# Masks on GpSimd for two of six units, squares on ScalarE, and late gathers one tile at a time, in a block-sparse attention with an expert router

## Chip, cores and metric

The kernel runs on one core of a Trainium2 chip. The metric is the device time of one execution in microseconds, as the median of several runs. A core has TensorE (PE; its weight loads are shown as PEld), VectorE (DVE), ScalarE (ACT), GpSimd (POOL) and SyncE (SP), which issues most DMAs.

## The reference, cut to what matters

Attention over 4 batches, 8 heads, 768 positions and head size 64, with a block mask, and then a router with 8 experts over the 3072 rows of 512 that it gives.

```python
scores = scale * q @ k.T                       # per batch and head, 768 x 768
scores = np.where(mask, scores, -1e9)          # mask by blocks of 32: window, first, last, random
attn = exp(scores - max) / (sum + 1e-9)
x = attn @ v                                   # -> (3072, 512)
xn = x / (norm(x) + 1e-6);  logits = xn @ en.T / tau
e = argmax(logits);  gate = softmax(logits)[e]
out = gate * (relu(x @ w1[e]) @ w2[e])         # w1: 512 x 1024, w2: 1024 x 512
```

## The kernel before

**Attention.** The work goes by pairs of heads: 16 pairs (4 per batch, index `g`), each of two halves of 384 queries, each half of six *units* `u` of 128 keys; `kc = u % 6`. Six units make one half `w = u // 6`; there are 192 units and 32 halves. For a unit, `score_fast` puts scores of both heads, keys on partitions, into PSUM: four bf16 matmuls add the mask (`kmask` by `qmask`, line 368, 0 or -1e9), and four groups of f32 matmuls add the product of `kt` and `qt` (line 368 too). ScalarE takes the exp of the 128x768 scores into a tile `e` (line 371; no maximum is subtracted, and a test at the end falls back to an exact version where sums are out of range). `attend_fast` multiplies `e` with `v` into `av` (line 390), and VectorE adds the `e` of a half up into `esum` (lines 385 and 387). At `kc` 5 ScalarE copies one half of `av` out (`part`, line 394) and VectorE adds the other (`at`, line 396).

Within a step, unit `u` is attended and then unit `u + 2` scored; at `kc` 0 the score comes first. The PSUM pool of scores has two buffers, the pool of `e` four.

`settle(w)` turns a half back to rows: small matmuls of `at` with an identity and the expert embedding (line 418), and of `esum` with ones for the row sums (line 425), into one PSUM tile `back`; VectorE adds the two halves of the sums (line 428), adds 1e-9 (429), takes the reciprocal (433), and writes the normed rows `x` (435) and the logits `part` (438). It is called at `kc` 3 of the following half. `squares(w)` at `kc` 4 squares and adds up 384 columns on GpSimd, one multiply (line 449) and seven adds of halving width (line 453); the last half uses ScalarE (line 463). The transposes of the next pair's `k` and `q` are VectorE operations at the first two units of a pair (line 285).

After each batch, steps of `route` (norms, logits, argmax, gate: lines 502 to 560) and `rank` are run between units at the places that `after_sequence` lists.

**Experts.** Rows are grouped by expert into tiles of 128. Five tiles (`NE`) are made of the first two batches, while attention still runs; the others ("late" tiles) after all rows are ranked. A tile is `hp = xgt @ w1` (line 891), relu by ScalarE for one half and VectorE for the other (894, 898), `yp = h @ w2` (904), scaling by the gate (912), and a scatter to the output by an indirect DMA from GpSimd's queue (913). The rows of a late tile are gathered by four indirect DMAs on that queue (line 812), two tiles ahead: `fetch(i)` calls `fetch_rows(i + 2)`. Weights come through SP's queue, 2 MB each (line 841).

In the first expert tile, `last_rows` settles the last half and routes the last batch in the middle of the tile. `between` then ranks and makes the slots of the late tiles in steps: `fill_slots` gives `slot_l` and, with four more matmuls (line 672), the indices `quarter` of the gathers.

The framework schedules each engine's instructions in program order by priority; `issue_after(x)` keeps what follows behind instruction `x`.

Of the kernel before, what the change touches and what calls it, by code (L numbers as in the profile page):

```python
# [19 lines left out]
P = 128  # L20
# [29 lines left out]
DEN_LOW, DEN_HIGH = 0.1, 1e10  # L50
NEG = -1.0e9


# [304 lines left out]
def score_fast(k, u):  # L358

    nc = k.nc  # L360
    g, qh, kc = u // (2 * NC), u // NC % 2, u % NC
    kt, qt = k.turned[g]
    ps = k.big.tile([P, 2, 512], F32, name="sc", tag="big")
    queries = slice(qh * HALF, (qh + 1) * HALF)
    quarters = [(h, r, slice(kc * P + D * r, kc * P + D * (r + 1))) for r in range(2) for h in range(2)]
    for rows, cols, first in ((k.kmask, k.qmask, True), (kt, qt, False)):
        for h, r, keys in quarters:
            nc.tensor.matmul(ps[D * r:D * (r + 1), h, 0:HALF], lhsT=rows[D * h:D * (h + 1), keys],  # L368
                             rhs=cols[D * h:D * (h + 1), queries], start=first, stop=not first)
    e = k.ep.tile([P, 2, HALF], F32, name="e", tag="e")  # L370
    k.exps = nc.scalar.activation(e, ps[:, :, 0:HALF], ACT.Exp, scale=SCALE)  # L371
    k.es[u] = e


# [25 lines left out]
def settle(k, w):  # L400
# [26 lines left out]
    den = k.dens[:, w, :]  # L427
    nc.vector.reduce_sum(out=den.rearrange("p (t h) -> p t h", t=NQ), in_=sums, axis=AX.X)
    nc.vector.tensor_scalar(out=den, in0=den, scalar1=1e-9, scalar2=None, op0=ALU.add)

# [11 lines left out]
def squares(k, w):  # L442

    nc = k.nc
    b, j, qh = w // (2 * NPAIR), w // 2 % NPAIR, w % 2
    chunks = slice(qh * NQ, (qh + 1) * NQ)
    x = k.x[b][:, chunks, j, 0:P]
    sq = k.sp.tile([P, NQ, P], F32, name="sq", tag="sq", bufs=1)
    nc.gpsimd.tensor_tensor(out=sq, in0=x, in1=x, op=ALU.mult)  # L449
    width = P // 2  # L450
    while width:
        out = sq[:, :, 0:width] if width > 1 else k.nsq[b][:, chunks, j:j + 1]
        k.squared = nc.gpsimd.tensor_tensor(out=out, in0=sq[:, :, 0:width], in1=sq[:, :, width:2 * width],  # L453
                                            op=ALU.add).ins
        width //= 2


def last_squares(k, w):

    b, j, qh = w // (2 * NPAIR), w // 2 % NPAIR, w % 2  # L460
    for c in range(qh * NQ, (qh + 1) * NQ):
        sq = k.sp.tile([P, P], F32, name="sq_l", tag="sq_l")
        k.nc.scalar.activation(sq, k.x[b][:, c, j, 0:P], ACT.Square,
                               accum_out=k.nsq[b][:, c, j:j + 1])
# [187 lines left out]

def fill_slots(k, lanes, val, nt, tiles, name, quarters=False):

    nc, p = k.nc, k.dp
    both = two_banks(k, "slot_ps")
    ps = both[:, 0, 0:2 * tiles]
    for t in range(nt):
# [7 lines left out]
    nc.vector.tensor_copy(out=slot, in_=got)  # L666
    if not quarters:
        return slot

    ps = both[:, 1, 0:NG * tiles].rearrange("p (g t) -> p g t", g=NG)  # L670
    for g in range(NG):
        nc.tensor.matmul(ps[:, g], lhsT=k.spread[:, g].rearrange("p e t -> p (e t)"), rhs=got, start=True, stop=True)
    k.quarter = k.const.tile([P, NG, tiles], I32, name="quarter")
    nc.vector.tensor_scalar(out=k.quarter, in0=ps, scalar1=float(ND), scalar2=k.group[:, 0:1], op0=ALU.mult,
                            op1=ALU.add)
    return slot

# [37 lines left out]
def dispatch_late(k):  # L715
# [63 lines left out]
    yield  # L779
    k.slots.append(fill_slots(k, k.lanes, val, NT, NL, "slot_l", True))  # L780
    yield
# [18 lines left out]
def fetch_rows(k, i):  # L800
# [5 lines left out]
    with ExitStack() as order:  # L806
        if k.squared is not None and not late:
            order.enter_context(k.tc.issue_after(k.squared))
        if late:
# [35 lines left out]
def fetch(k, i):  # L845

    if i + 2 < NE + NL:
        fetch_rows(k, i + 2)
    need = [(t, at) for t in range(NE + NL) for at in parts(t)]
    begin = [t for t, _ in need].index(i)  # L850
    for t, at in need[k.loads:begin + 3]:
        for _ in fetch_weights(k, t, at):
            pass
# [26 lines left out]

def expert_tile(k, i, meanwhile=None):
    nc = k.nc
# [4 lines left out]
    for f0 in (0, half):  # L887
# [5 lines left out]
        if f0 == 0:  # L893
            nc.scalar.activation(h[:, 0:half], hp, ACT.Relu)  # L894
            if meanwhile:
                meanwhile()
        else:
            k.relu = nc.vector.tensor_scalar(out=h[:, half:NF], in0=hp, scalar1=0.0, scalar2=None, op0=ALU.max).ins  # L898

    if i + 1 < NE + NL:  # L900
# [7 lines left out]
def finish(k, i, yp, gate, slot):  # L908
# [3 lines left out]
    nc.vector.tensor_scalar(out=y, in0=yp, scalar1=gate, scalar2=None, op0=ALU.mult)  # L912
    nc.gpsimd.indirect_dma_start(  # L913
        out=k.out[:, :], out_offset=bass.IndirectOffsetOnAxis(ap=slot, axis=0),
        in_=y[:, :], in_offset=None, bounds_check=N - 1, oob_is_err=False,
    )

# [56 lines left out]
def attention_fast(n, ctx):  # L974
# [3 lines left out]
    n.acc, n.big = pool("acc", 1, space=PSUM), pool("big_f", 2, space=PSUM)  # L978
    n.ld, n.tp, n.ep = pool("ld", 3), pool("tp", 2), pool("ep", 4)
    pairs = B * NPAIR  # L980
# [26 lines left out]
    load_pair(n, 1, (2,))  # L1007
    plan, experts = [], build_experts(n)
    for u in range(units):
        g = u // per  # L1010
        if u % per == 0 and g + 2 < pairs:
            load_pair(n, g + 2, (2,))
        if u % NC == 3 and NC < u < units - 2 * NC:
            settle(n, u // NC - 1)
        if u % NC == 4 and NC < u < units - 2 * NC:
            squares(n, u // NC - 1)
        if u in (2, 4, 7):
# [6 lines left out]
        for when, what in plan:  # L1024
            if when == u % (per * NPAIR):
                with n.tc.issue_after(n.summed.ins), n.tc.issue_after(n.exps.ins), n.tc.issue_after(n.tick.ins):
                    what()

        steps = [partial(attend_fast, n, u)] + ([partial(score_fast, n, u + 2)] if u + 2 < units else [])
        for step in reversed(steps) if u % NC == 0 else steps:  # L1030
            step()
        turn = u % per - (0 if g else NC - 1)
        if turn in (0, 1) and g + 1 < pairs:
# [45 lines left out]

def expert_tiles(n, between=(), first=None):  # L1080
    between = iter(between)
    for i in range(NE + NU):
# [6 lines left out]
        else:  # L1089
            expert_tile(n, i, first if i == 0 else None)  # L1090
        next(between, None)
    used = n.nc.values_load(n.used[0:1, 0:1], min_val=0, max_val=NL)
    with ExitStack() as more:
        for i in range(NU, NL):
            more.enter_context(n.tc.If(used > i))
            fetch(n, NE + i)
            expert_tile(n, NE + i)


def fast(n):  # L1100
    n.rings, n.loads, n.squared = {}, 0, None
    with ExitStack() as ctx:
# [10 lines left out]
        def between():  # L1113
            rank(n, B - 1)
            late = dispatch_late(n)
            next(late)
            yield
            yield
            next(late)
            count_good(n)  # L1120
            yield

        def last_rows():
            settle(n, 2 * B * NPAIR - 1)
            last_squares(n, 2 * B * NPAIR - 1)
            for _ in route(n, B - 1):
                pass

        expert_tiles(n, between(), last_rows)

# [92 lines left out]
```

## Time and profile before

| what | value |
|---|---|
| median of 3 runs | 697.7 us (697.24 to 698.05) |
| profiled execution, its own time | 701.82 us |
| span from first to last instruction in it | 700.1 us |
| granted TensorE clock, mean | 0.995 |
| attention ends about | 324 us |
| late expert tiles start about | 405 us |

The profile has, for groups of instructions by line and shape, the busy time, the mean of one in ns, and the engine's idle time before them with what ended it. The timeline has a start, a length (to the end of the last of the instructions merged in that line), the engine, the line, what is written and read, the number of instructions, and in brackets the idle time before it and its releaser. A table of stretches has for each engine the busy time and, in brackets, the instructions: PE, PEld, DVE, ACT, POOL, then the granted clock, the share of the DMA engines and GB/s. Matmuls of the four quadrants of the array run side by side, so a matmul's length is more than its share of TensorE's time.

### The profile page before, as it was taken

The page shows a single profiled execution, that of the slowest core. Times are in us where ns is not written, and L with a number is a line of the kernel's source. Part 1 is how long each engine was busy: PE and PEld are TensorE (multiplying, and loading weights), DVE is VectorE, ACT ScalarE, POOL GpSimd, SP SyncE. Part 2 cuts the span into 40 slices and gives each one's busy share as a digit, 9 for nine tenths or more (in the row PEclk, how much of TensorE's full clock was granted, in tenths as well). Part 3 has the DMA queues.
Part 4 walks back from the last instruction along what each step waited for, and adds up shares of the span by engine and source line. Part 5 has one row for each costly group of instructions (what it writes and reads, how often), then busy time and mean ns, then how long its engine had stood idle before and what let it go on. Part 6 is the DMA issues. An engine that isn't in the chain of part 4 may idle for free.

```text
span 700.1 us, 19413 instructions
## 1 busy us (share of the span) xinstructions
PE 683.5 (98%) x8237; PEld 449.7 (64%) x8237; DVE 345.2 (49%) x733; ACT 188.4 (27%) x266; POOL 296.3 (42%) x450
## 2 busy tenths in 40 slices
PE   9999999999999999999999899999999999999993
PEld 4777777555555555557767677766476665767771
DVE  6887778878788888765661111221112111221111
ACT  5455555554555455553000000000000001000000
POOL 1355466544774468535405543244323432241121
PEclk9999999999999999999999999999999999999997
DMA  7733344575326769643998799999899998999991
GB/s 122 131 66 52 49 70 70 131 161 100 64 41 163 128 159 209 225 153 132 329 408 306 284 402 322 342 349 336 291 390 414 404 377 303 418 396 416 326 330 51
DMA packets 172650, 164.87 MB, mean 235 GB/s; under 512 B 129340, under 2 KB 129340, under 8 KB 169478
## 3 DMA queue, kind: packets, MB, share of 16 engines
q1 hardware_dynamic: 165734, 149.86, 68.1%
q0 software_dynamic: 5216, 13.43, 5.4%
q8 instruction: 68, 1.11, 0.7%
q10 hardware_dynamic: 1600, 0.20, 0.2%
q14 instruction: 32, 0.26, 0.1%
HBM read 147.66 MB, written 16.07 MB: 234 GB/s over the span
## 4 chain that ended last, share of the span: by engine, by line
PE 93%; issue 2%; another core or an unknown queue 1%; DVE 1%; POOL 1%; ACT 0%; POOLq 0%
PE sc L368 22%; PE hp L891 21%; PE yp L904 21%; PE av L390 18%; PE back L425 3%; PE hp L932 2%; PE yp L952 2%; PE back L418 2%; PE warm L81 1%; POOL xg L812 0%; DVE row L938 0%; POOL nrm L514 0%; PE hp L944 0%; DVE h L898 0%
## 5 line engine op out<-in xcount | busy, mean ns | idle before, releaser
L371 ACT ACTIVATE e<-sc 128x768 f32<-128x768 f32 x192 | 155.5, 810 | 149.1 <-PE sc L368 147.3
L891 PEld LDWEIGHTS hp<-xgt,w 128*128 128x128 f32 x1472 | 168.1, 192 | 13.2 <-issue 12.6
L891 PE MATMUL hp<-xgt,w 128*128 128x128 f32 x1472 | 169.9, 276 | 2.0 <-issue 2.0
L904 PE MATMUL yp<-w,h 128*128 128x512 f32 x368 | 162.3, 593 | 1.2 <-DVE h L898 1.2
L368 PE MATMUL sc<-qt,kt 64*64 64x384 f32 x1536 | 162.7, 482 | 0.0
L390 PE MATMUL av<-e,vld 64*64 64x384 f32 x1536 | 158.9, 486 | 0.0
L812 POOL DMA_INDIRECT xg<-x_dram,quarter x88 | 88.2, 1003 | 140.4 <-DVE gate L877 101.5
L387 DVE TENSOR_TENSOR esum<-esum,e 128x768 f32<-128x768 f32 x128 | 129.3, 1010 | 34.4 <-ACT e L371 30.6
L904 PEld LDWEIGHTS yp<-w,h 128*128 128x128 f32 x368 | 68.0, 190 | 78.9 <-issue 75.8
L453 POOL TENSOR_TENSOR sq<-sq 128x192 f32<-128x192 f32 (+1 forms) x186 | 103.3, 555 | 13.9
L894 ACT ACTIVATE h<-hp 128x512 f32<-128x512 f32 x23 | 13.7, 597 | 295.9 <-PE hp L891 282.5
L390 PEld LDWEIGHTS av<-e,vld 64*64 64x64 f32 x1536 | 62.4, 133 | 47.2 <-issue 18.2
L368 PEld LDWEIGHTS sc<-qt,kt 64*64 64x64 f32 x1536 | 65.2, 133 | 32.3 <-issue 25.1
L898 DVE TENSOR_SCALAR h<-hp 128x512 f32<-128x512 f32 x23 | 15.9, 691 | 131.6 <-PE hp L891 122.0
L449 POOL TENSOR_TENSOR sq<-x 128x384 f32<-128x384 f32 x31 | 28.4, 918 | 115.6 <-DVE part L438 97.7
L368 PE MATMUL sc<-qmask,kmask 64*64 64x384 bf16 x768 | 71.6, 323 | 0.1
L912 DVE TENSOR_SCALAR y<-yp,gate 128x512 f32<-128x512 f32 x20 | 15.0, 751 | 101.0 <-PE yp L904 88.8
L368 PEld LDWEIGHTS <-kmask 64*64 64x64 bf16 x768 | 30.3, 107 | 27.4 <-issue 23.1
L913 POOL DMA_INDIRECT out_dram<-y,slot_l x20 | 20.2, 1009 | 63.0 <-DVE y L912 57.7
L385 DVE TENSOR_TENSOR esum<-e 128x768 f32<-128x768 f32 x32 | 31.3, 979 | 7.1 <-ACT e L371 7.0
L425 PE MATMUL back<-ones,esum 64*64 64x1 f32 x1536 | 27.4, 190 | 0.0
L425 PEld LDWEIGHTS back<-ones,esum 64*64 64x64 f32 x1536 | 26.5, 135 | 0.0
(204 smaller groups left out, 366.7 us busy)
## 6 DMA issues: line engine op xcount, KB each, us to landing
w<-in_moe_w_dram SPq DMA_DIRECT2D x54, 2048.0 KB
w<-in_moe_w_dram SPq DMA_DIRECT2D x16, 512.0 KB
x_dram<-x SPq DMA_DIRECT2D x24, 258.0 KB
vld<-in_v_dram SPq DMA_DIRECT2D x32, 192.0 KB
kld<-in_k_dram SPq DMA_DIRECT2D x60, 96.0 KB
qld<-in_q_dram SPq DMA_DIRECT2D x60, 96.0 KB
x_early<-x SPq DMA_DIRECT2D x12, 258.0 KB
xg<-x_dram,quarter POOLq DMA_INDIRECT x88
```

The lines of the kernel that those rows point to most:

```text
L368: nc.tensor.matmul(ps[D * r:D * (r + 1), h, 0:HALF], lhsT=rows[D * h:D * (h + 1), keys], rhs=cols[D * h:D * (h + 1), queries], start=first ...
L371: k.exps = nc.scalar.activation(e, ps[:, :, 0:HALF], ACT.Exp, scale=SCALE)
L385: k.summed = nc.vector.tensor_tensor(out=k.esum, in0=k.first, in1=e, op=ALU.add)
L387: k.summed = nc.vector.tensor_tensor(out=k.esum, in0=k.esum, in1=e, op=ALU.add)
L390: nc.tensor.matmul(k.av[D * h:D * (h + 1), r, 0:HALF], lhsT=v[D * r:D * (r + 1), h, kc, :], rhs=e[D * r:D * (r + 1), h, :], start=(kc == 0 ...
L425: nc.tensor.matmul(sums[D * s:D * (s + 1), t, h, r:r + 1], lhsT=esum[D * r:D * (r + 1), h, cols], rhs=k.ones[D * r:D * (r + 1), 0:1], star ...
L449: nc.gpsimd.tensor_tensor(out=sq, in0=x, in1=x, op=ALU.mult)
L453: k.squared = nc.gpsimd.tensor_tensor(out=out, in0=sq[:, :, 0:width], in1=sq[:, :, width:2 * width], op=ALU.add).ins
L812: k.nc.gpsimd.indirect_dma_start(out=x[:, g], out_offset=None, in_=quarters, in_offset=bass.IndirectOffsetOnAxis(ap=k.quarter[:, g, t:t + ...
L891: nc.tensor.matmul(hp[:, f, :], lhsT=w1[:, d, (f0 + f) * P:(f0 + f + 1) * P], rhs=xt[:, d, :], start=(d == 0), stop=(d == ND - 1))
L904: nc.tensor.matmul(yp, lhsT=h[:, f, :], rhs=w2[:, f, :], start=(f == 0), stop=(f == NF - 1))
L913: nc.gpsimd.indirect_dma_start(out=k.out[:, :], out_offset=bass.IndirectOffsetOnAxis(ap=slot, axis=0), in_=y[:, :], in_offset=None, bounds ...
```

## The change

- **Masks.** In units with `kc` 2 or 5, from the second pair on and except seven listed in `WHOLE`, the mask matmuls are left out. Instead GpSimd multiplies `e` in place by a 0/1 mask `cut` in bf16. `build_cut` makes this mask once, in the first half, from the same matmuls and a Relu. This makes 53 of 192 units.
- **Order.** Scores run three units ahead (`AHEAD`), the pool of `e` has five buffers, and `settle` comes at `kc` 2.
- **Squares** of all halves are three ScalarE operations with an accumulator, at `kc` 5.
- **Row sums.** The two halves of the sums are added by an addition of 1e-9 to the first and one of the second, both read from PSUM, in place of a reduction and an addition.
- **Late gathers.** The gathers of a late tile are issued after the latest scatter; those of the first late tile in the middle of expert tile 3, right after `spread_slots`, which is what was the second part of `fill_slots`.
- **Last route.** The routing of the last batch is put behind the VectorE relu of the first expert tile.

The core of the diff:

```diff
+AHEAD = 3
+CUT = (2, 5)
+WHOLE = {1: (11, 20), 2: (11, 20), 3: (11, 14, 20)}
...
 def score_fast(k, u):
...
-    for rows, cols, first in ((k.kmask, k.qmask, True), (kt, qt, False)):
+    cut = g > 0 and kc in CUT and u % (2 * NC * NPAIR) not in WHOLE.get(g // NPAIR, ())
+    for rows, cols, first in ((k.kmask, k.qmask, True), (kt, qt, False))[int(cut):]:
         for h, r, keys in quarters:
             nc.tensor.matmul(ps[D * r:D * (r + 1), h, 0:HALF], lhsT=rows[D * h:D * (h + 1), keys],
-                             rhs=cols[D * h:D * (h + 1), queries], start=first, stop=not first)
+                             rhs=cols[D * h:D * (h + 1), queries], start=first or cut, stop=not first)
...
+    if cut:
+        mask = k.cut[:, CUT.index(kc), queries].unsqueeze(1).broadcast_to([P, 2, HALF])
+        k.squared = nc.gpsimd.tensor_tensor(out=e, in0=e, in1=mask, op=ALU.mult).ins
     k.es[u] = e
+
+def build_cut(k, i):
...
+            nc.tensor.matmul(ps[D * r:D * (r + 1), h, 0:HALF],
+                             lhsT=k.kmask[rows, CUT[i] * P + D * r:CUT[i] * P + D * (r + 1)],
+                             rhs=k.qmask[rows, h * HALF:(h + 1) * HALF], start=True, stop=True)
+    nc.scalar.activation(k.cut[:, i].rearrange("p (h t) -> p h t", h=2), ps[:, :, 0:HALF], ACT.Relu, bias=1.0,
+                         scale=-10.0 / NEG)
...
 def settle(k, w):
...
-    nc.vector.reduce_sum(out=den.rearrange("p (t h) -> p t h", t=NQ), in_=sums, axis=AX.X)
-    nc.vector.tensor_scalar(out=den, in0=den, scalar1=1e-9, scalar2=None, op0=ALU.add)
+    per_row = den.rearrange("p (t h) -> p t h", t=NQ)
+    nc.vector.tensor_scalar(out=per_row, in0=sums[:, :, :, 0], scalar1=1e-9, scalar2=None, op0=ALU.add)
+    nc.vector.tensor_tensor(out=per_row, in0=sums[:, :, :, 1], in1=per_row, op=ALU.add)
...
 def squares(k, w):
...
-    nc.gpsimd.tensor_tensor(out=sq, in0=x, in1=x, op=ALU.mult)
-    width = P // 2
-    while width:
...
     for c in range(qh * NQ, (qh + 1) * NQ):
+        sq = k.sp.tile([P, P], F32, name="sq", tag="sq")
         k.nc.scalar.activation(sq, k.x[b][:, c, j, 0:P], ACT.Square,
                                accum_out=k.nsq[b][:, c, j:j + 1])
...
 def fetch_rows(k, i):
...
-        if k.squared is not None and not late:
-            order.enter_context(k.tc.issue_after(k.squared))
+        behind = k.scattered if late else k.squared
+        if behind is not None:
+            order.enter_context(k.tc.issue_after(behind))
...
 def fetch(k, i):
-    if i + 2 < NE + NL:
+    if i + 2 < NE + NL and i + 2 != NE:
         fetch_rows(k, i + 2)
...
 def finish(k, i, yp, gate, slot):
-    nc.gpsimd.indirect_dma_start(
+    k.scattered = nc.gpsimd.indirect_dma_start(
...
 def attention_fast(n, ctx):
-    n.ld, n.tp, n.ep = pool("ld", 3), pool("tp", 2), pool("ep", 4)
+    n.ld, n.tp, n.ep = pool("ld", 3), pool("tp", 2), pool("ep", 5)
...
-        if u % NC == 3 and NC < u < units - 2 * NC:
+        if (u % NC == 2 and u > 2 * NC or u == NC + 3) and u < units - 2 * NC:
             settle(n, u // NC - 1)
-        if u % NC == 4 and NC < u < units - 2 * NC:
-            squares(n, u // NC - 1)
+        if u in (3, 5):
+            build_cut(n, u // 2 - 1)
...
-        steps = [partial(attend_fast, n, u)] + ([partial(score_fast, n, u + 2)] if u + 2 < units else [])
+        scored = u + (AHEAD if u > NC else 2)
+        steps = [partial(attend_fast, n, u)] + [partial(score_fast, n, i) for i in range(ahead, min(scored + 1, units))]
+        ahead = scored + 1
...
+        if u % NC == 5 and NC < u < units - 2 * NC:
+            with n.tc.issue_after(n.exps.ins):
+                squares(n, u // NC - 1)
...
 def expert_tiles(n, between=(), first=None, then=None, spread=None):
+    def first_late():
+        if spread:
+            spread()
+        fetch_rows(n, NE)
...
-            expert_tile(n, i, first if i == 0 else None)
+            expert_tile(n, i, {0: first, NE - 2: first_late}.get(i), then if i == 0 else None)
...
         def last_rows():
             settle(n, 2 * B * NPAIR - 1)
-            last_squares(n, 2 * B * NPAIR - 1)
-            for _ in route(n, B - 1):
-                pass
+            squares(n, 2 * B * NPAIR - 1)
+        def last_route():
+            with n.tc.issue_after(n.relu):
+                for _ in route(n, B - 1):
+                    pass
```

## The prediction

> **What bounds the kernel now.** I read the engine totals first, then busy time by stretch, then TensorE's instructions in order of time in one steady stretch.
>
> ```profile
> PE 683.5 (98%) x8237; PEld 449.7 (64%) x8237; DVE 345.2 (49%) x733; ACT 188.4 (27%) x266; POOL 296.3 (42%) x450
> ...
> 20.00:330.00 310.00, 310.00 (x6050) 196.34 (x6043) 244.90 (x479) 160.79 (x218) 171.49 (x299) 1.00 0.53 113
> ...
> 370.00:405.00 35.00, 32.09 (x202) 23.17 (x201) 5.88 (x15) 1.19 (x2) 20.98 (x21) 1.00 0.81 294
> ```
>
> In the attention stretch (20 to 330 us) PE is busy without a gap; VectorE (third number) is busy 79%, ScalarE 52%, GpSimd 55%. Only PE work removed, or PE work delayed, moves the time there. Around 370 to 405 PE has 2.9 us of holes; later it is full again.
>
> ```profile
> 154.36 0.83 PE L368 MATMUL sc<-qt,kt 64*64 64x384 f32 x8
> 155.01 0.83 PE L390 MATMUL av<-e,vld 64*64 64x384 f32 x8
> 155.65 0.34 PE L368 MATMUL sc<-qmask,kmask 64*64 64x384 bf16 x4
> 155.82 0.82 PE L368 MATMUL sc<-qt,kt 64*64 64x384 f32 x8
> 156.46 0.34 PE L368 MATMUL sc<-qmask,kmask 64*64 64x384 bf16 x4
> ```
>
> The second column (time from first start to last end) overlaps with the next group; the price of a group is the distance between starts. A mask is 155.82-155.65 = 0.16 us, a score 0.645, an av 0.645. A settle takes 1.04 (back starts 151.03, the next av 152.07). Six units and a settle are 6x(0.645+0.645+0.16)+1.04 = 9.74; the trace shows 9.79 (two like av groups start at 157.27 and 167.06).
>
> Then the two engines that get and lose work:
>
> ```profile
> 154.54 0.83 POOL L449 TENSOR_TENSOR sq<-x 128x384 f32<-128x384 f32 x1 [5.17 <-DVE part L438]
> 154.71 1.47 DVE L387 TENSOR_TENSOR esum<-esum,e 128x768 f32<-128x768 f32 x1 [0.20 <-ACT e L371]
> ...
> 254.11 0.95 DVE L387 TENSOR_TENSOR esum<-esum,e 128x768 f32<-128x768 f32 x1
> 254.22 1.52 POOL L449 TENSOR_TENSOR sq<-x 128x384 f32<-128x384 f32 x1 [5.86 <-DVE part L438]
> ```
>
> The same two instructions take 0.83 and 0.95 when first and 1.52 and 1.47 when second: whoever comes second waits for the other's end (154.54+0.83 = 155.37; esum ends 0.81 after that).
>
> **What the Trainium skill says.** "SBUF — State Buffer", section "Who interferes with whom": a VectorE instruction with two SBUF inputs and a GpSimd instruction that reads SBUF exclude each other for the whole instruction; one with at most one SBUF input does not. The lines above agree. The settle's and at's VectorE work reads one side from PSUM; only the five esum adds of a period contend. "GPSIMD Engine Reference", section "3.1 Elementwise — side-by-side cycle accounting": about 2.6 cycles per element for two inputs; at its 1.2 GHz 768 elements are an estimated 1.66 us, about 1.8 with a fixed part. The trace is split: the in-place adds of L453 fit (192 elements 0.59 alone, 96 elements 0.38: 2.2 ns each), the multiply L449 does not (384 in 0.83).
>
> **The change, part by part.** The order of instructions of both programs, engine by engine, gives the counts.
>
> *Masks.* 53 units (26 with kc 2, 27 with kc 5) lose their mask matmuls: 53x0.16 = -8.5 us of PE. Building the 0/1 mask costs two groups of four such matmuls, +0.3; its two Relu of 128x768 (0.81 each like L371) lie on an idle ScalarE. In exchange 53 multiplies of 128x768 go to GpSimd, between exp and av. Their price is not in the trace. Low end, from the nearest row, L449 (a multiply of full rows): twice 0.83 less the fixed part (0.14, what an op that queued behind a lock saves) = 1.51. High end, the slope of L453: 768x2.2 ns + 0.17 = 1.85. I take 1.51, for it is the same operation; L453 adds in place. In-place writing and the bf16 mask could push it up.
>
> Does it fit? Scores now run three units ahead. Call 0 the start of the av of unit 5; exp starts 0.25 after its score (155.01 to 155.26) and takes 0.81, a successor starts 0.04 later, PE needs about 0.2 from release to first product (weights 0.15). Unit 2: score ends 1.29, multiply ready 2.39, av due 5.23, so 2.6 us are free. Unit 5: score ends 6.52, ready 7.62, av due 9.42: **1.60 us** free. 1.51 fits, barely, and only where no esum holds the port.
>
> VectorE's order in a period: at, esum of 0+1, esum 2, 3, 4, the five settle operations (1.31), esum 5; esums follow each other every 1.05 (0.95 and a gap). In a period without transposes: at 1.46-2.02, esum 0+1 to 3.0, multiply 2 waits for it and runs to 4.4, esum 2, 3, 4 end at 5.4, 6.4, 7.5, multiply 5 runs 7.62-9.13 under the settle: no stall. Every other period has four transposes (2.06): multiply 2 goes first (2.39-3.9), esum 0+1 ends 4.7, transposes to 5.75, esum 3 ends 7.8; multiply 5 waits for it, ends 9.2, PE is just in time. But esum 4, the settle and esum 5 end 2.9 us into the next period; there at, multiply 2 and all esums are late, esum 4 runs 7.25-8.2, multiply 5 ends 9.56, and av starts 9.78: 0.36 late. So 0.18 on average, 27x0.18 = +4.9. Ends: 0, if the port is luckier; at 1.85 the same working gives stalls of 0.25 to 1.0, mean 0.63, 27x0.63 = +17. Net of masks: -8.5+0.3+4.9 = **-3.3** (-8.2 to +8.8).
>
> *Squares.* The GpSimd chain of L449 and L453 (about 4.2 us per period) becomes three ScalarE squares, 1.0 us together by the last rows' L463 (first start 332.11, last end 333.10). They sit behind exp 2 and delay exp 3 to 4.16; its av is due after 5.9 and the next user of its PSUM buffer starts at 5.88: 0, covered by 1.7 us; uncovered 1 us per period. ScalarE goes to 6x0.81+0.47+1.0 = 6.3 of 9.4. Without this GpSimd could not hold two multiplies.
>
> *Row sums, settle sooner, fifth e buffer.* Two tiny VectorE operations replace two (L428 0.164, L429 0.165): 0. The settle moves ahead of av 2; it needs at (2.02, or 3.6 when late) and starts at 4.19: 0, and it is what gives unit 2 its slack. If VectorE fell 2 us later still, PE would wait for at. Five e buffers keep the distance between an exp and the esum it overwrites: 0.
>
> *Last route after the relu.* In tile 0 PE waited 0.3 for h L898, queued behind routing on VectorE: -0.3. The route then ends about 0.7 later; its oh was ready 2.5 us before the rank matmul (338.57 against 341.09): covered.
>
> *Gathers.* SP's queue is unchanged in order. On GpSimd, the late gathers (1.3 us from start to start) stood 14 in a row, from 373.89 to 391.86, ahead of the scatter of tile 3. Now four are issued, then a scatter, then four. The first four move from 373.9 to about 376.5, and are first used at 398.74: covered by over 15 us. What they free:
>
> ```profile
> 383.88 0.69 DVE L898 TENSOR_SCALAR h<-hp 128x512 f32<-128x512 f32 x1 [9.56 <-remote]
> ...
> 384.63 3.70 PE L904 MATMUL yp<-w,h 128*128 128x512 f32 x8 [0.94 <-DVE h L898]
> ...
> 392.39 0.47 PE L891 MATMUL hp<-xgt,w 128*128 128x128 f32 x2 [1.04 <-issue]
> 393.80 4.29 PE L891 MATMUL hp<-xgt,w 128*128 128x128 f32 x37 [0.94 <-issue]
> ```
>
> PE's three holes (last brackets) are 2.9 us. They lie within the row of 14, and later tiles, with four gathers each, have none. The cause is not named ("remote"), so this is a choice: **-2.9**, between 0 and -4.0 (hp of tiles 3, 4 and 5 starts at 371.43, 388.33, 404.96: two tiles of 16.9 and 16.6 against 14.0, less 1.5 of transposes and slot matmuls). In the steady tiles a gather behind a scatter is used over 15 us later: 0. The tail from the last yp (688.1) to the end is untouched.
>
> Sum: -3.3-0.3-2.9 = -6.5. The profiled execution took 701.8 (span 700.1 and 1.7 around it), so 695.3; the median of the runs is 697.7, 4.1 below it, so **691.2**.
>
> **Rivals.**
> 1. *GpSimd becomes the bound* (slower). If the multiply costs what the adds do, 1.85, av of unit 5 waits 0.63 on average: 697.7+8.8-0.3-2.9 = 703.3. It decides from the point where multiply and port wait exceed about 2.0 us (1.60, plus 0.31 saved per period, plus 3.2/27). For it: L453, the skill's price, the 1.52 above. Against: L449.
> 2. *All hidden.* Transposes and port waits fall luckily, no stall: 697.7-8.2-0.3-2.9 = 686.3; with the whole 4.0, 685.2.
> 3. *The holes stay.* They come from something else than the gathers (weights in flight, the same on SP's queue): 697.7-3.3-0.3 = 694.1.
>
> **How the numbers follow.** Forecast 0.42 (own range 688 to 696), rival 1 0.33, rival 2 0.13, rival 3 0.12. Seven of the hundred, from stalls near the break-even, I count within 0.2%, about what a measurement of this kernel can tell from no change (696.3 to 699.1): faster 0.60, same 0.07, slower 0.33. The range takes rival 2 and most of rival 1: 685 to 704.
>
> **What would show it.** Right: the multiply near 1.5 us where no esum overlaps; PE's wait before av, named after the multiply, near 5 us in all; six units 9.4 to 9.8 apart; no holes from 370 to 405. Wrong: a median of the multiply above 1.8, PE waiting 0.5 us or more in most periods for the multiply (rival 1), waits of a score for exp (squares in the way), or of settle for at (VectorE late).

## Result and the profile after

The changed kernel takes **724.1 us** (median of 6 runs, 722.06 to 724.74) against 697.75 for the kernel before beside it: ratio 1.0373, 95% interval 1.0359 to 1.0387. The forecast was 691.2, with a range of 685 to 704. The profiled execution has a span of 722.4 us. The expert stage starts at 351.67 us instead of 324.59: attention takes **27.1 us more**. What follows it takes 370.7 us, against 371.7 in the profile of the kernel before that stands at the median (before_third, below).

First the same totals as before, then busy time by stretch (PE, PEld, VectorE, ScalarE, GpSimd, clock, DMA share, GB/s), both of the changed kernel.

```profile
PE 686.0 (95%) x8033; PEld 426.3 (59%) x8033; DVE 376.2 (52%) x733; ACT 214.8 (30%) x454; POOL 252.1 (35%) x255
```

```profile
20.00:345.00 325.00, 303.13 (x5622) 165.04 (x5618) 270.79 (x469) 181.72 (x389) 124.41 (x102) 0.99 0.45 104
...
397.00:432.00 35.00, 35.00 (x239) 27.14 (x238) 6.54 (x15) 1.79 (x3) 12.67 (x13) 1.00 0.89 316
```

PE now has 22 us without work in the attention stretch, where it had none. GpSimd is busy for 124 us, less than before: it is no bound by its own time. VectorE's busy time up to the end of attention grew from 258 to 288 us, with as many adds as before; about 18 us of that are in the 32 first adds of the halves (979 to 1541 ns on average) and about 4 in the other 128 adds. The waits of that stretch (20 to 345 us; total, times, longest) say for what PE stood. A weight load (PEld) can wait while PE still works; idle time of PE itself is in the lines of PE:

```profile
PEld av L416 <- DVE at L422: 31.7, 29, 2.6
...
DVE esum L413 <- POOL e L381: 22.4, 15, 2.9
...
PE av L416 <- DVE at L422: 16.2, 13, 1.9
PEld av L416 <- POOL e L381: 15.4, 27, 1.3
```

So it stood for `at`, and for the multiply only 1.1 us in all. In the kernel before, `at` of a half with transposes starts 1.5 us and ends 2.0 us after the av of unit 5 (174.59), and PE doesn't stand for it:

```profile
176.05 0.56 DVE L396 TENSOR_TENSOR at<-av,part 128x384 f32<-128x384 f32 x1 [0.51 <-ACT part L394]
```

One half of the changed kernel in order of time shows what became of it (start, length, engine, line):

```profile
155.17 1.65 POOL L381 TENSOR_TENSOR e<-e,cut 128x768 f32<-128x768 f32 x1 [2.59 <-ACT e L378]
...
155.54 2.10 DVE L411 TENSOR_TENSOR esum<-e 128x768 f32<-128x768 f32 x1
...
157.56 1.02 DVE L291 STREAM_TRANSPOSE qt<-qld 128x384 f32<-128x384 f32 x2
...
158.52 4.43 DVE L413 TENSOR_TENSOR esum<-esum,e 128x768 f32<-128x768 f32 x3
...
160.49 1.65 POOL L381 TENSOR_TENSOR e<-e,cut 128x768 f32<-128x768 f32 x1 [3.67 <-ACT e L378]
...
162.19 0.88 PE L416 MATMUL av<-e,vld 64*64 64x384 f32 x8
...
162.88 0.15 DVE L456 TENSOR_SCALAR dens<-back 128x6 f32<-128x6 f32 x1
...
163.48 0.56 DVE L463 TENSOR_TENSOR x<-back,inv 128x384 f32<-128x384 f32 x1
...
164.07 0.95 DVE L413 TENSOR_TENSOR esum<-esum,e 128x768 f32<-128x768 f32 x1
...
164.94 0.55 DVE L422 TENSOR_TENSOR at<-av,part 128x384 f32<-128x384 f32 x1
...
165.54 1.52 PE L416 MATMUL av<-e,vld 64*64 64x384 f32 x16 [1.02 <-DVE at L422]
```

The add of units 0 and 1 takes 2.10 us instead of 0.95, because the multiply, which began earlier, holds the SBUF port that both engines need till 156.82; the second multiply stretches the three next adds from about 3.05 (0.95 each, 1.05 apart) to 4.43. The settle's five operations and the last add follow, and `at` ends 3.3 us after the av of unit 5 began. The next half's first av may not write before `at` has read, for the pool of `av` has one buffer. PE is 1.02 us late.

The distance from one half's first exp to the next one's, summed over 31 halves against the kernel before, splits the loss (24.7 of the 27.1 us):

| halves | number | difference |
|---|---|---|
| without transposes (9.79 before, 9.49 to 9.56 in most) | 16 | -3.3 |
| with transposes (9.79 before, 10.7 to 11.0 in most) | 11 | +10.1 |
| with transposes and `rank` (10.3 to 10.7 before, 13.3 to 16.5) | 4 | +17.8 |

So a half saves its two masks (0.30) where VectorE has room, and halves with transposes are 1.3 us longer than those without (10.8 against 9.5 us). The four routed halves are the larger part of the loss. An estimated 3.4 us of it is TensorE's clock, which was at half in two stretches of 3.41 us (last section); how the rest divides was not worked out. In them PE also waits for the settle; its own waits in the same stretch have these two:

```profile
PE rk L581 <- DVE part L466: 2.7, 3, 0.9
PE slot_ps L670 <- DVE part L466: 1.8, 1, 1.8
```

`rank` comes in the step of `kc` 2, where the settle now is, and so do the early slots; all three write the one PSUM tile `small`.

### The profile page after: what moved, and what is told of

Same layout as the page of the kernel before. It is cut to its first block, busy times and chain, and to the rows that moved or that the text cites. A ratio compares the mean times of both kernels' runs of the same rounds, so it can differ in the third digit from the quotient of the medians.

```text
span 722.4 us, 19013 instructions
## 1 busy us (share of the span) xinstructions
PE 686.0 (95%) x8033; PEld 426.3 (59%) x8033; DVE 376.2 (52%) x733; ACT 214.8 (30%) x454; POOL 252.1 (35%) x255
## 4 chain that ended last, share of the span: by engine, by line
PE 69%; DVE 21%; issue 3%; ACT 3%; DMA 2%; POOL 1%; SPq 0%; DVEq 0%; POOLq 0%; ACTq 0%
PE hp L908 22%; PE yp L923 21%; PE sc L375 9%; DVE esum L413 9%; PE av L416 9%; DVE esum L411 3%; PE hp L951 2%; PE yp L971 2%; ACT e L378 2%; DVE kt L291 2%; PE back L451 1%; DVE x L463 1%; DVE qt L291 1%; DMA out_dram<-y,slot_l 1%; DVE at L422 1%
## 5 line engine op out<-in xcount | busy, mean ns | idle before, releaser
L416 PE MATMUL av<-e,vld 64*64 64x384 f32 x1536 | 164.7, 496 | 18.0 <-DVE at L422 16.5
L908 PEld LDWEIGHTS hp<-xgt,w 128*128 128x128 f32 x1472 | 167.8, 192 | 10.8 <-issue 10.8
L375 PE MATMUL sc<-qt,kt 64*64 64x384 f32 x1536 | 169.7, 486 | 0.0
L381 POOL TENSOR_TENSOR e<-e,cut 128x768 f32<-128x768 f32 x53 | 92.6, 1748 | 204.1 <-ACT e L378 204.1
L413 DVE TENSOR_TENSOR esum<-esum,e 128x768 f32<-128x768 f32 x128 | 133.0, 1039 | 35.9 <-POOL e L381 24.7
L416 PEld LDWEIGHTS av<-e,vld 64*64 64x64 f32 x1536 | 54.2, 134 | 83.4 <-issue 33.7
L375 PE MATMUL sc<-qmask,kmask 64*64 64x384 bf16 x556 | 52.1, 326 | 0.1
L411 DVE TENSOR_TENSOR esum<-e 128x768 f32<-128x768 f32 x32 | 49.3, 1541 | 0.2 <-ACT e L378 0.2
L375 PEld LDWEIGHTS <-kmask 64*64 64x64 bf16 x556 | 20.9, 108 | 22.6 <-issue 22.1
L475 ACT ACTIVATE sq<-x 128x128 f32<-128x128 f32 x96 | 28.3, 299 | 8.6 <-DVE x L463 8.5
L422 DVE TENSOR_TENSOR at<-av,part 128x384 f32<-128x384 f32 x32 | 17.7, 554 | 16.9 <-ACT part L420 16.9
```

The costliest lines, as they stand in the source:

```text
L381: k.squared = nc.gpsimd.tensor_tensor(out=e, in0=e, in1=mask, op=ALU.mult).ins
L411: k.summed = nc.vector.tensor_tensor(out=k.esum, in0=k.first, in1=e, op=ALU.add)
L413: k.summed = nc.vector.tensor_tensor(out=k.esum, in0=k.esum, in1=e, op=ALU.add)
L416: nc.tensor.matmul(k.av[D * h:D * (h + 1), r, 0:HALF], lhsT=v[D * r:D * (r + 1), h, kc, :], rhs=e[D * r:D * (r + 1), h, :], start=(kc == 0 ...
L422: k.summed = nc.vector.tensor_tensor(out=at, in0=k.av[:, 0, 0:HALF], in1=part, op=ALU.add)
L908: nc.tensor.matmul(hp[:, f, :], lhsT=w1[:, d, (f0 + f) * P:(f0 + f + 1) * P], rhs=xt[:, d, :], start=(d == 0), stop=(d == ND - 1))
```

## Experiments

"Attention ends" is the start of the first `hp`; it hardly differs between chips for the same kernel (324.1 to 324.6 in three profiles of the kernel before). Ratios are to the kernel before on the same chip.

| run | time, us | ratio (95%) | attention ends |
|---|---|---|---|
| changed kernel | 724.1 | 1.0373 (1.0359 to 1.0387) | 351.7 |
| expert_only | 699.33 | 1.0019 (1.0012 to 1.0026) | 324.7 |
| expert_only_again | 699.37 | 1.0024 (1.0016 to 1.0033) | 324.6 |
| no_cut | 702.55 | 1.0064 (1.0047 to 1.0080) | 329.6 |
| settle_kc3 | 718.43 | 1.0288 (1.0271 to 1.0305) | 346.1 |
| turns_apart | 714.75 | 1.0236 (1.0210 to 1.0262) | 342.3 |
| mult_aside | (attention only) | | 353.2 |
| half_mult | (attention only) | | 328.3 |
| settle_after | 737.34 | 1.0493 (1.0471 to 1.0515) | 363.9 |
| settle_after_turns | 738.42 | 1.0506 (1.0484 to 1.0528) | 365.4 |
| settle_after2 | 719.79 | 1.0315 (1.0298 to 1.0332) | 346.4 |
| turns_kc3 | 704.98 | 1.0105 (1.0088 to 1.0122) | 331.9 |
| turns_kc3_cut2 | 699.92 | 1.0022 (1.0014 to 1.0030) | 327.2 |
| turns_kc3_cut14 | 699.06 | 1.0016 (1.0009 to 1.0023) | 325.5 |
| turns_kc3_cut1 | **696.23** | **0.9979** (0.9972 to 0.9986) | 322.9 |

### Which part of the change costs: no_cut

```diff
-    cut = g > 0 and kc in CUT and u % (2 * NC * NPAIR) not in WHOLE.get(g // NPAIR, ())
+    cut = False
```

`build_cut` and the order behind `n.squared` are left out with it.

> The changed kernel with all masks on TensorE again (no multiply by GpSimd, no 0/1 mask built); settle at kc 2, scores three ahead, five e buffers, ScalarE squares, row sums from PSUM and the expert stage stay. Theory 1 (the multiplies' share of the SBUF port makes VectorE late, and 'at' holds the next half's av) and theory 2 (the multiplies themselves are late for av): the whole loss goes, halves 9.8 and routed halves about 10.7, 697.7 - 4.3 = 693.4. Theory 3 (settle at kc 2 meets rank and the slots in the one PSUM tile 'small'): the four or five routed halves keep holes of 0.9 to 1.8 us and some clock, 696 to 703. Theory 4 (squares on ScalarE delay the exps): over 0.3 us per half stays, above 703.

702.55, inside the range of theory 3. Attention ends at 329.6, so the multiplies with their saved masks account for 22.1 of the 27.1 us and the rest of the change for **5.0**. The unrouted halves after the second take 9.79 as before: the ScalarE squares, the row sums and the fifth `e` buffer cost nothing there, and theory 4 falls. The four routed halves take 1.3 to 1.5 more each, 5.6 us in all. PE's waits of no_cut (20 to 345 us) hold these two:

```profile
PE rk L581 <- DVE part L466: 2.4, 3, 0.8
PE slot_ps L670 <- DVE part L466: 0.8, 1, 0.8
```

Theory 3 is right for that part: the settle one step sooner takes `small` from `rank` and the slots. These waits are 3.2 of the 5.6 us; the rest is not taken apart, and the early settle was not run without the other edits.

### Port or product: mult_aside and half_mult

```diff
-        k.squared = nc.gpsimd.tensor_tensor(out=e, in0=e, in1=mask, op=ALU.mult).ins
+        aside = k.sp.tile([P, 2, HALF], BF16, name="aside", tag="aside", bufs=1)
+        k.squared = nc.gpsimd.tensor_tensor(out=aside, in0=e, in1=mask, op=ALU.mult).ins
```

(`part` gets two buffers instead of three, for room.)

> The changed kernel, but the multiply writes its product to a tile that nobody reads (bf16), so that the masks of the 53 units are left out. GpSimd works and holds the SBUF port as before, but nobody waits for its result. Port theory (the multiply's hold on the port stretches VectorE's adds until 'at' is late): most of the loss stays, 712 to 722, esum of 0+1 still near 1.55 us. Waiting theory (the adds of units 2 and 5, and what queues behind them on VectorE, wait for the product): the loss goes but for the routed halves' 5 us of the early settle, 694 to 698.

Attention ends at 353.2, no earlier than in the changed kernel. Without masks rows are routed otherwise and the expert stage runs more tiles, so only attention is read. The group of the first adds of mult_aside from 20 to 345 us (busy time, mean in ns, idle time before), and its wait of av:

```profile
L412 DVE TENSOR_TENSOR esum<-e 128x768 f32<-128x768 f32 x31 | 46.9, 1514 | 0.0
```

```profile
PE av L417 <- DVE at L423: 20.6, 13, 3.2
```

Nobody reads a product here, and the add of units 0 and 1 still takes 1514 ns (980 in the kernel before; 1560 in the changed kernel), and av still waits for `at`. The half shown above looks the same in it:

```profile
158.44 4.51 DVE L414 TENSOR_TENSOR esum<-esum,e 128x768 f32<-128x768 f32 x3
...
165.54 1.52 PE L417 MATMUL av<-e,vld 64*64 64x384 f32 x16 [1.12 <-DVE at L423]
```

Halves with transposes take 10.7 to 11.0 in most, in both kernels. **The hold on the port alone gives a loss of this size**; no wait for the masked `e` is needed for it. One wait of another kind remains in this run: in 13 places an exp waited for the multiply to have read the buffer that it overwrites, 8.3 us in all, but PE's holes stand before av.

```diff
-        mask = k.cut[:, CUT.index(kc), queries].unsqueeze(1).broadcast_to([P, 2, HALF])
-        k.squared = nc.gpsimd.tensor_tensor(out=e, in0=e, in1=mask, op=ALU.mult).ins
+        mask = k.cut[:, CUT.index(kc), queries]
+        k.squared = nc.gpsimd.tensor_tensor(out=e[:, 0], in0=e[:, 0], in1=mask, op=ALU.mult).ins
```

> The changed kernel, but each multiply covers one of the two heads (384 columns, near 0.83 us), so that half of the masks of the 53 units are left out. If the hold on the port is what makes VectorE late, halving it removes more than half of the holes, since VectorE then has slack: attention ends near 333 (routed halves keep their 5 us of the early settle). If a fixed cost of each multiply matters and not its length: near 351.

328.3, better than expected: every unrouted half but a few falls to 9.49, and PE's wait for `at` from 16.2 to 3.1 us. The multiplies are as many as in the changed kernel, and each takes 0.92 us alone instead of 1.65. The hold is shorter and the product is also earlier; mult_aside says which of the two matters. With half the hold VectorE is in time in nearly every unrouted half.

### Room on VectorE: turns_apart, settle_kc3, turns_kc3

turns_apart (in the first pair as before):

```diff
-        turn = u % per - (0 if g else NC - 1)
+        turn = u % per // NC if g and u % NC == 0 else u - NC + 1 if not g else -1
```

> The changed kernel with the four transposes of the next pair split: the two of k in the first half of a pair, the two of q in the second (1.03 us of VectorE in every half instead of 2.06 in every other). Theory 1: halves of 10.8 to 11.0 and 9.5 become about 9.6 each, 13 us less outside the routed halves: about 711; the idle time of av named after 'at' falls by half or more. Theory 2 (the multiply of unit 5 alone is too long for av): 724. Theory 3: 724.

Attention is 9.4 us shorter (13 were expected), unrouted halves are 9.5 to 9.9 in most, and PE's wait for `at` falls to 5.0 us. Theory 2 gave no difference. The routed halves stay at 12.9 to 15.7.

```diff
-        if (u % NC == 2 and u > 2 * NC or u == NC + 3) and u < units - 2 * NC:
+        if u % NC == 3 and NC < u < units - 2 * NC:
```

> The changed kernel with settle at kc 3 again, as before the change; all else stays. Theory 3: rank and the slots get the PSUM tile without waiting for settle, the routed halves fall from 13.3 to 16.5 towards 11.7, 4 x 3 us: about 712. Theory 1: VectorE's queue is as full as it was, and settle's VectorE work only comes later: 724 or slower, to 735. Theory 2: 724.

5.6 us, half of what theory 3 gave. The waits of `rank` and slots are gone, and the last two routed halves fall by 4.0 and 2.6 us; the first two still take 14.6 and 16.3, and there PE stands longest for `at`, 2.2 us each of 18.0 in all. TensorE's clock was at half for 10.2 us in this profile, 3.4 more than in the changed kernel, which hides an estimated 1.7 us of the gain.

turns_kc3 has both edits.

> The changed kernel with the transposes split over both halves of a pair and settle at kc 3. If the two repairs add up (9.8 and 5.6 us of attention): attention ends near 336.3. If they repair the same wait: near 342.

331.9, 19.8 us less where the sum was 15.0. The surplus is the clock: it was at half for 6.8 us in the profiles of the changed kernel and of turns_apart, for 10.2 in settle_kc3, and never in turns_kc3. Counting half of these times as lost, an estimate, the edits give 9.4 and 7.3 alone and 16.4 together, so they about add up. The first two routed halves fall to 12.3 only with both.

### The order of the settle and `at`: settle_after, settle_after_turns, settle_after2

The settle after the step of `kc` 5, behind `at`:

```diff
-        if (u % NC == 2 and u > 2 * NC or u == NC + 3) and u < units - 2 * NC:
-            settle(n, u // NC - 1)
...
-        if u % NC == 5 and NC < u < units - 2 * NC:
+        if u % NC == 0 and 2 * NC <= u <= units - 2 * NC:
             with n.tc.issue_after(n.exps.ins):
-                squares(n, u // NC - 1)
+                squares(n, u // NC - 2)
+        if u % NC == 5 and NC < u < units - 2 * NC:
+            with n.tc.issue_after(n.summed.ins):
+                settle(n, u // NC - 1)
```

> The changed kernel with settle called after the step of kc 5, so that its five VectorE operations stand behind 'at' and not ahead of it, and the squares one step later; nothing else. Theory 1 ('at' late in VectorE's queue holds the next half's av): 'at' is 1.3 us earlier in every half, its waits of 18 to 31 us nearly vanish, 700 to 707. Theory 2 (the product of unit 5 is late for av): 724. Theory 3 (rank meets settle): that part alone, 718.

A miss: attention ends 12 us later than in the changed kernel, where some 20 less were expected. PE's waits for `at` are gone, but those of settle_after from 20 to 345 us show others:

```profile
ACT sq L475 <- DVE x L463: 67.5, 28, 3.3
...
DVE esum L413 <- POOL e L381: 51.9, 33, 2.5
...
PE sc L375 <- ACT e L378: 29.6, 23, 1.9
```

ScalarE stands at the squares until VectorE has written `x`, the exps stand behind the squares, and PE behind the exps. That is the edit's own fault: the squares were only one step behind the settle. settle_after_turns, with the transposes split as well, has the same waits.

> The same and the transposes split over both halves of a pair. Theory 1: no wait for 'at' left outside the routed halves, halves of 9.5: 695 to 702. Theory 2: 724. If the time is then still above 702, a third thing delays 'at' or av.

settle_after2 puts the squares at `kc` 2 and the route's first step one later.

> As settle_after, but the squares two steps later still (kc 2) and the route's first step one later, so that ScalarE need not wait for the rows x. If theory 1 (VectorE's order keeps 'at' late) is right and settle_after only failed because ScalarE stood waiting for x and held the exps: no wait of av for 'at' and none of ScalarE for x, attention ends near 335 (351.7 in the changed kernel, 363.9 in settle_after). If moving settle behind 'at' is itself at fault: above 352.

346.4: better than the changed kernel by 5.2 us, not by 16.7. No wait of PE for `at` remains, but others have come in its place (settle_after2, same stretch):

```profile
ACT sq L475 <- DVE x L463: 19.1, 17, 2.1
...
PE av L416 <- POOL e L381: 13.6, 23, 1.0
```

With the settle's work moved to the front of the half, av waits for the multiply instead. In one half of its trace the squares wait 1.21 us for `x` (till 159.90), the exp of unit 5 comes behind them, the multiply starts at 161.72, right behind that exp, and av at 163.41, after 0.78 us of idle time. So in this half it is the late squares again; for the other halves this is not shown. Theory 1 in its narrow form (only the place of `at` is wrong) falls; with the two runs on the port, what holds is that two holds per half, with the settle at `kc` 2 and four transposes in one half, leave VectorE too little room.

### How many multiplies, and where: cut2, cut1, cut14

All three start from turns_kc3. Only `kc` 2 is cut:

```diff
-    cut = g > 0 and kc in CUT and ...
+    cut = g > 0 and kc == 2 and ...
```

> The same with only the units of kc 2 cut (26 multiplies). Port theory: half the hold on the port, halves of 9.65 (one mask of 0.16 less than 9.81) with the holes nearly gone; attention ends near 324 to 326, against 324.6 in the kernel before. If one multiply is already too much: above 328.

Unrouted halves are 9.65 to 9.69, as expected, and no hole of PE is named after `at` or the multiply; attention ends 1.2 us later than expected. One routed half takes 13.05, with the clock at half for 3.41 us. That doesn't happen in every execution: nine of the 20 took 697.5 to 698.7 us with a mean clock of 0.993 to 0.996, and eleven 699.9 to 700.6 with 0.991.

With `CUT = (1, 4)`, `kc == 1`, and seven such units in routed halves left whole (23 multiplies):

> The same with only units of kc 1 cut, and those of the routed halves left whole. This multiply runs while VectorE does the transposes, which have one SBUF input, so by the port theory it holds up fewer adds than that of kc 2: esum of 0+1 near 1.0 us, attention ending 1 to 3 us earlier than with kc 2, near 322 to 324. If only the number of multiplies counts: the same as with kc 2.

322.9, in the range that was expected of the place. But the unrouted halves take 9.62 to 9.68, the same as with `kc` 2: with one multiply VectorE has room either way. The 4.3 us between the two are nearly all in routed halves, where this kernel has fewer multiplies and its clock never fell, so this pair does not show what the place is worth. It does show what the place does to an add. VectorE and GpSimd in one half of turns_kc3_cut2, in order of time:

```profile
157.23 1.03 DVE L291 STREAM_TRANSPOSE qt<-qld 128x384 f32<-128x384 f32 x2
...
157.72 1.66 POOL L381 TENSOR_TENSOR e<-e,cut 128x768 f32<-128x768 f32 x1 [8.00 <-ACT e L378]
...
158.18 2.01 DVE L411 TENSOR_TENSOR esum<-e 128x768 f32<-128x768 f32 x1
```

And of turns_kc3_cut1:

```profile
155.44 1.65 POOL L381 TENSOR_TENSOR e<-e,cut 128x768 f32<-128x768 f32 x1 [7.97 <-ACT e L378]
...
155.77 0.56 DVE L422 TENSOR_TENSOR at<-av,part 128x384 f32<-128x384 f32 x1 [1.83 <-ACT part L420]
...
156.25 1.03 DVE L291 STREAM_TRANSPOSE qt<-qld 128x384 f32<-128x384 f32 x2
...
157.20 0.92 DVE L411 TENSOR_TENSOR esum<-e 128x768 f32<-128x768 f32 x1
```

In the second `at` and the transposes run inside the multiply at their own length, and the add of units 0 and 1 follows it in 0.92 us. "SBUF — State Buffer" of the Trainium skill, section "Who interferes with whom", says so of VectorE instructions with at most one SBUF input, outside its two-port modes. From 20 to 335 us that add takes 928 ns on average in cut1 and 1597 in cut2. This kernel is faster than the kernel before by 1.4 us, 0.2%: 696.23 us.

> Two multiplies per half again, now for kc 1 and kc 4, with the transposes split and settle at kc 3; nine units of routed halves left whole. If it counts where the multiply meets the adds: that of kc 1 meets the transposes and that of kc 4 an add, so attention ends between that of kc 1 alone (322.9) and that of kc 2 and 5 (331.9), near 325. If only the number counts: near 332.

325.5, where "near 325" was expected. `WHOLE` leaves eleven units here, not nine, which makes 49 multiplies. Against turns_kc3 this is the pair that tests the place: two multiplies per half in both, a full clock in both, and the 19 halves away from routing are 4.5 us shorter together (9.46 to 9.64 in most, against 9.49 to 9.90). The first adds take 936 ns on average instead of 1471. Against turns_kc3_cut1, the halves in and beside routing (10.3 to 11.5 in most) take back more than the second multiply saves.

### The expert stage: expert_only, before_again, before_third

The hunks of the expert stage alone (`fetch`, `fetch_rows`, `spread_slots`, `finish`, `expert_tile`, `expert_tiles`, `last_route`) on the kernel before.

> The kernel before with only the changes of the expert stage (gathers of one late tile at a time, the last route behind the relu, the quarter indices made in a step of their own). If the expert stage's 4.3 us (last yp minus end of attention, changed kernel against before) come from these edits and not from the later end of attention: 697.7 - 4.3 = 693.4, tiles 3 and 4 near 15.8 and 14.0 instead of 16.9 and 16.6, no holes of PE from 370 to 400, attention ending at 324.6 as before. If the holes only went because the stage started later: 697.7.

699.33: 1.4 us slower. Its last yp starts at 683.9 us, 4.2 earlier than in the profile that the prediction read, but that profile is not the usual one; on which chip it was taken is not on record.

> The kernel before, profiled once more. Its first profile stood 4.1 us above the median of its runs. If the three holes of PE and the two slow tiles of 374 to 395 us belong to every execution: span near 696 and tiles of 16.9 and 16.6 us again, and then the kernel with only the expert stage changed should not be as slow as before. If they belong to that one execution: span near 696, these tiles at 15.8 and 14.0, no holes, and the gathers' edit has nothing to gain.

This chip gave 702.5 us for the kernel before, and tiles of 17.0 and 17.0 us.

> The kernel before, profiled a third time. If the holes of 374 to 395 us and the slow tiles 3 and 4 come with the chip: on a chip whose time of the kernel before is near 697.7 they are absent (tiles near 15.8 and 14.0, last yp near 684), on one near 702.5 they are there (near 17 us each).

On this one it took 697.6, and tiles 3 and 4 are 15.7 and 14.0. The stretch from 370 to 405 us of before_again and of before_third:

```profile
370.00:405.00 35.00, 32.01 (x200) 23.12 (x200) 5.89 (x14) 1.19 (x2) 20.52 (x21) 1.00 0.82 290
```

```profile
370.00:405.00 35.00, 35.00 (x242) 27.36 (x241) 6.54 (x15) 1.79 (x3) 23.05 (x23) 1.00 0.95 334
```

The program is the same, and one has the holes and the other none. The DMA engines moved 290 GB/s in one and 334 in the other; why that chip is slower there is not known.

> The kernel before with only the expert stage's changes, beside that profile. If the new order of the gathers is worth what the holes cost: on a chip near 702.5 it gains 2.6 to 4.2 us, on one near 697.7 nothing (699.3 there before, with 1.6 us more in the last instructions after the last scatter).

699.37, on the chip of before_third. Tile 0 is 0.35 us shorter (16.52 against 16.87), the others are equal within 0.1. The 1.5 us come at the very end: in both profiles of this kernel GpSimd's queue, which has nothing but semaphore instructions left, stops for 1.6 to 1.9 us between two of them (the step takes 0.04 in the others). No other kernel here has it. Do the new gathers gain where the holes are? Three of the kernels with the new order ran on the chip of before_again, mult_aside, settle_after and settle_after_turns, and there tiles 3 and 4 of settle_after take 15.8 and 14.0 us, 4.2 less than in before_again. Their attention ended 29 to 41 us later, so the order of the gathers wasn't tried alone there; on the chips with the usual time it gains nothing.

## Why the prediction was wrong

- **Masks, -8.5: right.** Halves with room became 9.49 from 9.79, the 0.31 of the working.
- **Price of the multiply, 1.51 taken, up to 1.85: between.** 1.64 to 1.65 alone, 1748 ns on average with what it waits for. The working's other estimate, 1.66, was nearest. L449 misled: half_mult has this multiply on as many columns, 384, at 0.92 us, against 0.83 for L449, so the two are not the same operation in price. (L449 does fit the price per element behind the 1.66, which the working denied: half of 1.66 is 0.83.) Not what decided.
- **Stalls of av 5 behind the multiply, +4.9: the step that failed.** PE waited 1.1 us for the multiply in all, and 16.2 us for `at`. The working had followed VectorE to `at` at 3.6 us after the av of unit 5 in every other half (measured 3.3), and then compared it with the settle at 4.19. The next half's first av is due at about 2.3 (162.19 to 164.52) and needs the same `at`, since the tile `av` has one buffer. From 3.6 less 2.3 the same working would have given 1.3 us in every other half; 1.02 of idle time was measured, in halves 1.3 us longer than those without transposes. "If VectorE fell 2 us later still, PE would wait for at" named the right wait with the wrong deadline.
- **Settle sooner, 0: failed.** Without the multiplies attention still takes 5.0 us more (no_cut), and of the halves that it leaves longer by more than 0.1 us all four are routed; 3.2 us are PE's waits for the settle by a PSUM tile that the working didn't follow. Routed halves, 17.8 us of the loss, weren't worked out at all. Their own two-input operations on VectorE grow with the multiplies too: that of line 544 takes 939 ns on average in the changed kernel and 207 in no_cut.
- **Squares on ScalarE, row sums, fifth buffer, 0: right** (no_cut's halves of 9.79).
- **Last route, -0.3: right** as far as tile 0 shows it, -0.35 to -0.57; it wasn't run alone.
- **Gathers, -2.9: failed** for the time that was forecast, and with it the conversion to the median. The profiled execution stood 4.1 us above the median, and before_third, at the median, has no holes: as far as these profiles show, the holes were in that execution and not in those near the median. Taking off the 4.1 and then the 2.9 counted the same time twice.
- The sum: multiplies +22.1, the rest of attention +5.0, last route -0.4, gathers 0 give 26.7; 26.4 were measured.
- **Rivals.** Rival 1 had the side, and the wrong mechanism: GpSimd isn't the bound and its product is not what PE waits for. Rival 2 didn't happen: stalls cost more than the masks saved. Rival 3 had the outcome of the gathers, for another reason.

## To carry to other kernels

When work is put on GpSimd beside a VectorE that is busy 80%, count what its hold on the SBUF port takes from VectorE's adds, and then follow VectorE's queue to every reader with a deadline: a result that frees a single-buffered PSUM tile is due at that tile's next writer. Put the held time under VectorE instructions that have at most one SBUF input; here the next add took 928 ns when the multiply lay under the transposes and 1597 when the two met. That shortens the kernel only where VectorE is short of room: with two multiplies per half it did, with one it made no difference. Where a profiled execution is slower than the median of the runs, find where before a hole in it is counted as a gain.

## What was not expected of the hardware

- Chips differ in one stage: the kernel before took 702.6 us on one chip and 697.6 to 697.9 on the others, nearly all of it in the expert stage (4.5 us between two profiles), while attention ended within 0.5 us.
- After a hole of 1.93 us PE's granted clock fell to half for 3.4 us:

```profile
206.00:208.00 2.00, 0.59 (x8) 0.41 (x12) 2.00 (x4) 1.62 (x7) 1.77 (x4) 0.96 0.00 0
208.00:210.00 2.00, 2.00 (x20) 0.76 (x15) 1.79 (x3) 0.00 (x0) 1.31 (x2) 0.50 0.03 8
210.00:212.00 2.00, 2.00 (x64) 1.24 (x60) 0.36 (x1) 0.50 (x1) 0.00 (x0) 0.69 0.00 0
```

After another hole of the same length, which ended at 122.53, it stayed at 1.00. What decides was not settled; it is part of the routed halves' loss (16.0 against 14.3, where the clock stayed). The changed kernel's profile has a second such stretch in the half that takes 16.5.
